# Three running sums of a hidden quarter written back into their PSUM banks, and their low halves formed from there

## The chip, the cores and the metric

The kernel runs on one core of a Trainium2 chip. The metric is the device time of one execution in microseconds. The kernel before takes 2179.87 us (median of three runs, 2179.35 to 2181.54).

## What is computed

Sparse attention over 4 batches, 8 heads, 768 positions and a head width of 64 feeds a mixture of 8 experts on 3072 tokens of width 512. The expert weights of every token come from a gate that is balanced eight times. The change lies in the expert part:

```python
def _moe_ref(x, w_gate, w1, w2):
    ...                                   # P: the balanced gate, tokens x experts
    for e in range(E):                    # 8 experts
        h = np.maximum(x @ w1[e], 0.0)    # 3072 x 512 by 512 x 1024
        ye = h @ w2[e]                    # 3072 x 1024 by 1024 x 512
        out += P[:, e:e + 1] * ye
```

## The kernel before

The attention comes first (to about 550 us, with the first expert work from about 400 us between), then the experts. Expert work is cut into 32 items `i`, one for each expert and batch, and an item into four quarters `qi` of 128 hidden rows. Every float32 factor is held as two float16 parts, a high half and a low half, and one product is three matmuls for each slice (high by high, high by low, low by high).

**First layer, `stage1(i, qi)`.** x @ w1 is a 2x2 block product done with seven products instead of eight. For a quarter, `product(p)` puts product p into one PSUM bank, a tile named `p`: six matmuls of 384 columns (line 1580). The products come in the order 0, 1, 5, 6, 3, 4, 2; from item 8 on product 0 is not done here but is itself split into seven smaller products by `fine` (tiles `fx`, `fy`, `fz`), one item ahead. The banks come from the pool `ps_h`, which has four for all of these; a second pool of four banks, `ps_y`, serves the second layer (tiles `py`).

VectorE's `comb` (line 1485) adds a product to a running sum. The running sums are `a1`, `r11`, `u3` and `c21`, float32 tiles in SBUF of 128x384. Four of them end as blocks of the hidden layer: `r11` after product 1, `c21` after product 3, `u3` after product 4, `a1` after product 2. Each then gets its ReLU on ScalarE (lines 1630, 1663, 1650, 1655).

**Halves of h.** The second layer is a 2x2 block product too, so it needs seven left factors, h 0 to 6. Three are blocks themselves (h 0 from `r11`, h 1 from `c21`, h 3 from `u3`); h 6, 5, 4 and 2 are sums and differences of blocks, which `add` makes on GpSimd (line 1658 and, through `sub`, 1298). `emit(p, src)` makes the two float16 halves: the high half on ScalarE (line 1596), the low half as source minus high half. The low half is done on GpSimd where p is in `LOPE`, else on VectorE, as a TENSOR_TENSOR (both line 1607), or, where `relu=True` is given, as a SCALAR_TENSOR_TENSOR that takes the ReLU along (line 1601).

**Second layer, `stage2(i, p)`.** 36 matmuls of 256 columns (line 1710) for each p, in three groups of 12, in the order 1, 0, 5, 6, 3, 4, 2. The results are added to the output by VectorE (line 1734).

**What sets the order.** The items are interleaved: `stage2` of item i runs between the products of `stage1` of item i + 1. Small work (low halves, sums, the split of the next expert's weights, lines 1276 on ScalarE, 1280 on VectorE, 1291 on GpSimd) waits in the queues of `Slots`, which gives it out by due steps and by planned costs on each engine (`dve=`, `act=`, `pool=`). After that a scheduler of the framework sets the final order on each engine, and it decides which freed bank a new tile of a pool gets.

Of the kernel before, what the change touches and what calls it, by code (L numbers as in the profile page):

```python
# [15 lines left out]
AF = mybir.ActivationFunctionType  # L16
# [18 lines left out]
LGAT = 400  # L35
NU = 8
LOP = (2, 3)
LOPE = (2, 3, 5)
NLE = 99
LEADS, LAGS = (1.0, 1.0, 1.0), (1.0, 1.0, 1.0)  # L40
SD = (2, 3, 4, 5)
# [15 lines left out]
def tile_sparse_attention_moe(  # L57
# [11 lines left out]
    nc = tc.nc  # L69
# [394 lines left out]
    with ExitStack() as actx:  # L464
        pool = lambda name, bufs, **kw: actx.enter_context(
            tc.tile_pool(name=name, bufs=bufs, reuse_waits="tile", **kw)
        )
# [795 lines left out]
    slots = Slots()  # L1263
# [33 lines left out]
    def sub(out, x, y):  # L1297
        nc.gpsimd.tensor_tensor(out=out, in0=x, in1=y, op=ALU.subtract)  # L1298
# [185 lines left out]
    def comb(t, ps, other):  # L1484
        nc.vector.scalar_tensor_tensor(  # L1485
            out=t, in0=ps, scalar=HDOWN, in1=other, op0=ALU.mult, op1=ALU.add
        )
# [83 lines left out]
    def stage1(i, qi, used=None):  # L1571
        fs = slice(qi * P, (qi + 1) * P)
        lop = LOPE if i < NLE else LOP

        def product(p):
            slots.need(("w1", i // B, p))
            ps = ps_h.tile([P, 512], F32, tag="ph", name=f"p{p}_{i}_{qi}")[:, :TH]
            for kc in range(KH):
                for m, (l, r) in enumerate(((0, 0), (0, 1), (1, 0))):
                    nc.tensor.matmul(  # L1580
                        ps, lhsT=w1ps[i // B][p][:, l, kc, fs], rhs=xp[p][:, r, kc],
                        start=(kc == 0 and m == 0), stop=(kc == KH - 1 and m == 2),
                    )
            if used and p in used:
                used[p]()
            return ps

        def fresh(nm):
            return upool.tile([P, TH], F32, tag="u", name=f"{nm}_{i}_{qi}")

        def emit(p, src, relu=False, delay=0):
            key = ("h", i, p), i, qi

            def high():
                h = hs[i, p, qi] = hfree.pop(0)
                nc.scalar.activation(h[:, 0], src, AF.Relu if relu else AF.Copy)  # L1596

            def low():
                h = hs[i, p, qi]
                if relu:  # L1600
                    nc.vector.scalar_tensor_tensor(
                        out=h[:, 1], in0=src, scalar=0.0, in1=h[:, 0],
                        op0=ALU.max, op1=ALU.subtract,
                    )
                else:
                    eng = nc.gpsimd if p in lop else nc.vector
                    eng.tensor_tensor(out=h[:, 1], in0=src, in1=h[:, 0], op=ALU.subtract)  # L1607

            if delay:
                slots.add(high, key, delay, act=0.52)  # L1610
            else:
                high()
            if p in lop:
                slots.add(low, key, delay, pool=0.95)
            else:
                slots.add(low, key, delay + 1, dve=0.6 if relu else 0.78)

        def tick(n, m):
            slots.tick(0.976, 0.55 * n, 0.5 * m)

        if i < FIRST_FINE:
            a1 = fresh("a1")
            nc.scalar.activation(a1, product(0), AF.Copy, scale=HDOWN)
            tick(0, 1)
            yield
        else:
            a1 = pairs[i][qi // 2][:, qi % 2]
        r11 = fresh("r11")
        comb(r11, product(1), a1)
        nc.scalar.activation(r11, r11, AF.Relu)  # L1630
        emit(0, r11)
        tick(1, 2)
        yield
        comb(a1, product(5), a1)
        tick(1, 0)
        yield
        u3 = fresh("u3")
        comb(u3, product(6), a1)
        tick(1, 0)
        yield  # L1640
        slots.settle(i, qi - 1)
        c21 = fresh("c21")
        comb(c21, product(3), u3)
        emit(1, c21, relu=True)
        tick(1, 1)
        yield
        p5 = product(4)
        comb(u3, p5, u3)
        comb(a1, p5, a1)
        nc.scalar.activation(u3, u3, AF.Relu)  # L1650
        emit(3, u3)
        tick(2, 2)
        yield
        comb(a1, product(2), a1)
        nc.scalar.activation(a1, a1, AF.Relu)  # L1655

        def add():
            nc.gpsimd.tensor_tensor(out=s1, in0=a1, in1=u3, op=ALU.add)  # L1658
            sub(a1, a1, r11)
            slots.need((("h", i, 0), i, qi))  # L1660
            sub(r11, s1, r11)
            slots.need((("h", i, 1), i, qi))
            nc.scalar.activation(c21, c21, AF.Relu)
            sub(c21, c21, r11)

        s1 = fresh("s1")
        slots.add(add, (("sum", i), i, qi), 1, act=0.52, pool=4.3)
        emit(4, s1, delay=SD[0])
        emit(6, a1, delay=SD[1])
        emit(5, r11, delay=SD[2])  # L1670
        emit(2, c21, delay=SD[3])
        tick(1, 1)
        yield
# [100 lines left out]
    parts = split_w2(0, wr[2])  # L1774
    parts[0]()
    run(stage1(0, 0))
    for part in parts[1:]:
        part()
    for qi in range(1, FH // P):
        if qi == FH // P - 1:  # L1780
            slots.need(("w2", 0, 1))
        run(stage1(0, qi))
# [6 lines left out]
    def products(i):  # L1789
        def swap(i):  # L1790
            e, b = divmod(i, B)
            return follows[e + 1] if b == B - 1 and e + 1 < NE else None

        if i == FIRST_FINE:
            for _ in fine(i, swap(i)):
                yield 3
        ahead = fine(i + 1, swap(i + 1)) if FIRST_FINE <= i < NI - 1 else None
        for qi in range(FH // P):
            for _ in stage1(i, qi, swap(i) if qi == FH // P - 1 else None):
                yield 2  # L1800
                if ahead and qi >= QFINE and next(ahead, "end") != "end":
                    yield 0
        if ahead:
            for _ in ahead:
                yield 0
# [91 lines left out]
```

## Time and profile before

| | |
|---|---|
| median of three runs | 2179.87 us |
| the profiled execution | 2178.01 us |
| its span on the core | 2176.2 us |
| TensorE matmuls | 2131.4 us busy |
| VectorE | 1793.5 us busy |
| GpSimd | 1481.0 us busy |
| ScalarE | 1278.7 us busy |

The profile lists, for each engine, how long it was busy and what ended its idle time. TensorE's weight loads (PEld) overlap its matmuls (PE). A group of instructions is named by its line, its engine, and the tiles that it writes and reads: `h<-r,h` on line 1607 is the low half made from `r11`.

### The profile page before, as it was taken

To read this page: it belongs to the slowest core of one execution; us is meant where nothing else is said; L and a number is where in the kernel's file an instruction comes from. 1 tells how busy PE (TensorE), PEld (TensorE's weight loads), DVE (VectorE), ACT (ScalarE), POOL (GpSimd) and SP (SyncE) were. 2 spreads that over 40 slices of the span, in tenths; PEclk is the share of its full clock that TensorE was granted. 3 is DMA by queue.
4 is the path that set the end of the run, shared out by engine and by line. 5 is a ranking of instruction groups with operands and counts; after the bars stand their busy time and mean duration, and the time that the engine had idled before them with its cause. 6 is when DMAs were issued, how large, how long until landed. Compare 5 with 4: busy or idle time off the path is not lost.

```text
span 2176.2 us, 48599 instructions
## 1 busy us (share of the span) xinstructions
PE 2131.4 (98%) x19228; PEld 1617.1 (74%) x19228; DVE 1793.5 (82%) x3116; ACT 1278.7 (59%) x2352; POOL 1481.0 (68%) x1550
## 2 busy tenths in 40 slices
PE   6999999999999999999999999999999999999999
PEld 4777776677777777777777777777777777777777
DVE  8889988777878787878787878787878887888775
ACT  5888888766465656555555555555555555555442
POOL 5667778578558775867586758675867586758553
PEclk9999999999999999999999999999999999999999
DMA  6857795142144434343434343434343434343331
GB/s 172 190 127 176 172 214 139 50 135 103 56 155 143 149 117 163 124 155 117 155 117 156 117 156 117 156 117 155 117 155 117 155 117 156 117 156 124 117 103 52
DMA packets 208313, 293.11 MB, mean 135 GB/s; under 512 B 133820, under 2 KB 152276, under 8 KB 200916
## 3 DMA queue, kind: packets, MB, share of 16 engines
q1 hardware_dynamic: 207520, 289.97, 42.4%
q8 instruction: 150, 2.46, 0.5%
q14 instruction: 79, 0.65, 0.1%
q10 hardware_dynamic: 564, 0.03, 0.0%
HBM read 195.59 MB, written 62.91 MB: 119 GB/s over the span
## 4 chain that ended last, share of the span: by engine, by line
PE 67%; DVE 14%; POOL 11%; issue 5%; ACT 4%; DMA 0%; POOLq 0%; DVEq 0%; ACTq 0%
PE py L1710 29%; PE p L1580 24%; PE u L834 3%; POOL h L1607 2%; PE t L769 2%; PE t L772 2%; PE m L736 2%; PE m L739 2%; DVE h L1607 2%; POOL s L1658 2%; DVE top L745 2%; POOL r L1291 1%; DVE acc L1734 1%; DVE w2p L1280 1%; DVE a L1485 1%
## 5 line engine op out<-in xcount | busy, mean ns | idle before, releaser
L1710 PEld LDWEIGHTS <-h 128*128 128x128 f16 x8064 | 787.4, 98 | 155.7 <-issue 9.0
L1710 PE MATMUL py<-w2p,h 128*128 128x256 f16 x4608 | 573.7, 273 | 1.0 <-ACT acc L1731 0.7
L1607 POOL TENSOR_TENSOR h<-u,h 128x384 f16<-128x384 f32 x128 | 135.5, 1059 | 448.6 <-ACT h L1596 448.2
L1710 PE MATMUL py<-vault,h 128*128 128x256 f16 x3456 | 411.2, 273 | 5.2 <-DVE vault L1280 3.1
L1734 DVE SCALAR_TENSOR_TENSOR acc<-py,spare,acc 128x256 f32<-128x256 f32 (+1 forms) x588 | 297.3, 513 | 70.8 <-PE py L1710 64.4
L1596 ACT ACTIVATE h<-c 128x384 f16<-128x384 f32 x256 | 133.0, 521 | 303.4 <-DVE c L1485 232.0
L1580 PEld LDWEIGHTS <-attic 128*128 128x128 f16 x2016 | 196.7, 98 | 104.5 <-issue 0.2
L1485 DVE SCALAR_TENSOR_TENSOR a<-p,a 128x384 f32<-128x384 f32 x384 | 210.8, 549 | 23.6 <-PE p L1580 17.1
L1580 PE MATMUL p<-attic 128*128 128x384 f16 x1152 | 214.4, 326 | 0.0
L745 DVE TENSOR_REDUCE top<-m 128x1 f32<-128x768 f32 x192 | 182.0, 950 | 30.8 <-PE m L739 29.7
L777 ACT ACTIVATE pe<-t,qk 128x768 int32<-128x768 f32 x192 | 172.4, 900 | 57.8 <-PE t L772 45.3
L1580 PEld LDWEIGHTS <-arena 128*128 128x128 f16 x1440 | 140.4, 98 | 77.9 <-issue 4.2
L1658 POOL TENSOR_TENSOR s<-a,u 128x384 f32<-128x384 f32 x128 | 153.7, 1201 | 54.5 <-ACT a L1655 54.2
L1580 PEld LDWEIGHTS <-w1p 128*128 128x128 f16 x1344 | 131.0, 98 | 71.5 <-issue 2.0
L1607 DVE TENSOR_TENSOR h<-s,h 128x384 f16<-128x384 f32 x128 | 114.5, 895 | 68.2 <-ACT h L1596 66.7
L1298 POOL TENSOR_TENSOR c<-c,r 128x384 f32<-128x384 f32 x128 | 158.1, 1235 | 10.0
L1580 PE MATMUL p<-arena,attic 128*128 128x384 f16 x864 | 161.8, 326 | 0.0
L1596 ACT ACTIVATE h<-s 128x384 f16<-128x384 f32 x128 | 66.8, 522 | 161.7 <-POOL s L1658 161.5
L1298 POOL TENSOR_TENSOR r<-s,r 128x384 f32<-128x384 f32 x128 | 153.4, 1199 | 10.0
L1596 ACT ACTIVATE h<-r 128x384 f16<-128x384 f32 x256 | 130.7, 518 | 49.6 <-POOL r L1298 46.4
L1580 PE MATMUL p<-arena 128*128 128x384 f16 x864 | 159.2, 326 | 0.4 <-DVE u L1485 0.2
L791 POOL TENSOR_SCALAR pl<-pe 128x768 f16<-128x768 uint16 x126 | 109.0, 867 | 66.7 <-ACT pe L777 57.9
(239 smaller groups left out, 4732.0 us busy)
## 6 DMA issues: line engine op xcount, KB each, us to landing
arena<-xd SPq DMA_DIRECT2D x128, 384.0 KB, 4.0
accd<-acc SPq DMA_DIRECT2D x28, 1536.0 KB, 5.7
acc<-accd SPq DMA_DIRECT2D x28, 1536.0 KB, 6.5
attic<-xd SPq DMA_DIRECT2D x96, 384.0 KB, 3.7
r<-in_moe_w_dram SPq DMA_DIRECT2D x14, 2048.0 KB, 8.7
xpf<-xfd SPq DMA_DIRECT2D x24, 384.0 KB, 3.1
arena<-in_q_dram SPq DMA_DIRECT2D x16, 384.0 KB, 4.0
arena<-in_k_dram SPq DMA_DIRECT2D x16, 384.0 KB, 4.8
```

The source lines that it names most:

```text
L745: nc.vector.tensor_reduce(out=tops[n][:, c : c + 1], in_=sc[:, :S], axis=AX.X, op=ALU.max)
L777: nc.scalar.activation(pe, sc[:, :S], AF.Exp, bias=EXP_SHIFT, scale=qk[n // 2][3])
L791: nc.gpsimd.tensor_scalar(lo, low, FINE, 1.0, ALU.mult, ALU.mult)
L834: nc.tensor.matmul(uv[:, c, :n], lhsT=l[:, c * P : (c + 1) * P], rhs=w[:, h, kc, :n], start=(kc == 0 and c == 0 and m == 0), stop=(kc == N ...
L1298: nc.gpsimd.tensor_tensor(out=out, in0=x, in1=y, op=ALU.subtract)
L1485: nc.vector.scalar_tensor_tensor(out=t, in0=ps, scalar=HDOWN, in1=other, op0=ALU.mult, op1=ALU.add)
L1580: nc.tensor.matmul(ps, lhsT=w1ps[i // B][p][:, l, kc, fs], rhs=xp[p][:, r, kc], start=(kc == 0 and m == 0), stop=(kc == KH - 1 and m == 2),)
L1596: nc.scalar.activation(h[:, 0], src, AF.Relu if relu else AF.Copy)
L1607: eng.tensor_tensor(out=h[:, 1], in0=src, in1=h[:, 0], op=ALU.subtract)
L1658: nc.gpsimd.tensor_tensor(out=s1, in0=a1, in1=u3, op=ALU.add)
L1710: nc.tensor.matmul(py, lhsT=hs[i, p, kc][:, l, tsl], rhs=w2p[p][:, r, kc], start=(old is None and kc == 0 and m == 0), stop=(kc == KF // 2 ...
L1734: nc.vector.scalar_tensor_tensor(out=dst, in0=src, scalar=c, in1=dst, op0=ALU.mult, op1=ALU.add)
```

## The change

`comb` now writes three of the four finished sums into the PSUM bank that it has just read: the sum of product 1 (until now `r11`), of product 3 (`c21`) and of product 4 (`u3`). High and low halves of h 0, 1 and 3 are formed from the bank, both with the ReLU taken along, and a separate ScalarE instruction puts the ReLU of the sum into the SBUF tile that `add` reads later. The ReLU of `c21` is issued at once and no longer inside `add`. At product 4 the two sums change places, since the one in place has to come second. `LOPE` goes from (2, 3, 5) to (2, 5, 6): the low half of h 3 moves from GpSimd to VectorE, that of h 6 from VectorE to GpSimd. Two planned costs are adapted.

```diff
-LOPE = (2, 3, 5)
+LOPE = (2, 5, 6)
...
-                slots.add(low, key, delay + 1, dve=0.6 if relu else 0.78)
+                slots.add(low, key, delay + 1, dve=0.56 if relu else 0.78)
...
         r11 = fresh("r11")
-        comb(r11, product(1), a1)
-        nc.scalar.activation(r11, r11, AF.Relu)
-        emit(0, r11)
+        p2 = product(1)
+        comb(p2, p2, a1)
+        emit(0, p2, relu=True)
+        nc.scalar.activation(r11, p2, AF.Relu)
         tick(1, 2)
...
         c21 = fresh("c21")
-        comb(c21, product(3), u3)
-        emit(1, c21, relu=True)
-        tick(1, 1)
+        p3 = product(3)
+        comb(p3, p3, u3)
+        emit(1, p3, relu=True)
+        nc.scalar.activation(c21, p3, AF.Relu)
+        tick(1, 2)
         yield
         p5 = product(4)
-        comb(u3, p5, u3)
         comb(a1, p5, a1)
-        nc.scalar.activation(u3, u3, AF.Relu)
-        emit(3, u3)
+        comb(p5, p5, u3)
+        nc.scalar.activation(u3, p5, AF.Relu)
+        emit(3, p5, relu=True)
         tick(2, 2)
...
             slots.need((("h", i, 1), i, qi))
-            nc.scalar.activation(c21, c21, AF.Relu)
             sub(c21, c21, r11)
...
-        slots.add(add, (("sum", i), i, qi), 1, act=0.52, pool=4.3)
+        slots.add(add, (("sum", i), i, qi), 1, pool=4.3)
```

On VectorE, in a plain quarter (item 16, from the low half of h 1 in quarter 1 to product 6 of quarter 2; in `p4_16_1_...` 4 is the product, 16 the item, 1 the quarter), there stood before:

```order
L1601 SCALAR_TENSOR_TENSOR h_5_8119<-c21_16_1_19108,h_5_8119 128x384
L1734 SCALAR_TENSOR_TENSOR acc_1_8145<-py_15_0_1_18932,spare_6_16783,acc_1_8145 128x512
L1485 SCALAR_TENSOR_TENSOR u3_16_1_19082<-p4_16_1_19134,u3_16_1_19082 128x384
L1485 SCALAR_TENSOR_TENSOR a1_16_0_18535<-p4_16_1_19134,a1_16_0_18535 128x384
L1485 SCALAR_TENSOR_TENSOR a1_16_0_18535<-p2_16_1_19146,a1_16_0_18535 128x384
L1734 SCALAR_TENSOR_TENSOR acc_1_8145<-py_15_0_2_18955,spare_6_16783,acc_1_8145 128x512
L1485 SCALAR_TENSOR_TENSOR r11_16_2_19176<-p1_16_2_19177,a1_16_1_18536 128x384
L1607 TENSOR_TENSOR h_8_8122<-s1_16_1_19155,h_8_8122 128x384
L1734 SCALAR_TENSOR_TENSOR acc_1_8145<-py_15_3_0_19189,spare_6_16783,acc_1_8145 128x256
L1607 TENSOR_TENSOR h_24_8138<-a1_16_0_18535,h_24_8138 128x384
L1485 SCALAR_TENSOR_TENSOR a1_16_1_18536<-p5_16_2_19220,a1_16_1_18536 128x384
L1607 TENSOR_TENSOR h_15_8129<-r11_16_2_19176,h_15_8129 128x384
```

and now:

```order
L1601 SCALAR_TENSOR_TENSOR h_5_8119<-p3_16_1_19109,h_5_8119 128x384
L1485 SCALAR_TENSOR_TENSOR a1_16_0_18535<-p4_16_1_19135,a1_16_0_18535 128x384
L1485 SCALAR_TENSOR_TENSOR p4_16_1_19135<-p4_16_1_19135,u3_16_1_19082 128x384
L1485 SCALAR_TENSOR_TENSOR a1_16_0_18535<-p2_16_1_19147,a1_16_0_18535 128x384
L1601 SCALAR_TENSOR_TENSOR h_4_8118<-p4_16_1_19135,h_4_8118 128x384
L1736 SCALAR_TENSOR_TENSOR acc_1_8145<-py_15_0_2_18955,spare_6_16784,acc_1_8145 128x512
L1485 SCALAR_TENSOR_TENSOR p1_16_2_19177<-p1_16_2_19177,a1_16_1_18536 128x384
L1607 TENSOR_TENSOR h_8_8122<-s1_16_1_19156,h_8_8122 128x384
L1736 SCALAR_TENSOR_TENSOR acc_1_8145<-py_15_3_0_19189,spare_6_16784,acc_1_8145 128x256
L1601 SCALAR_TENSOR_TENSOR h_15_8129<-p1_16_2_19177,h_15_8129 128x384
L1485 SCALAR_TENSOR_TENSOR a1_16_1_18536<-p5_16_2_19220,a1_16_1_18536 128x384
```

The low half from `a1` (`h_24`) is gone from VectorE, that of h 3 (`h_4`) has come, and the low halves of h 0 and h 3 read the banks `p1` and `p4`, one or three rows after the sum was written there.

At a change of expert (the first quarters of item 17, while the second layer of item 16 runs with new weights) VectorE also splits w2: `w2p_6` and `vault_110` on line 1280 are the low halves of the weights for products 6 and 5 of the second layer. Before:

```order
L1485 SCALAR_TENSOR_TENSOR a1_17_0_19208<-p2_17_0_19712,a1_17_0_19208 128x384
L1280 SCALAR_TENSOR_TENSOR w2p_6_8110<-r2_4_18992,sw2_4_18997,w2p_6_8110 128x1024
L1280 SCALAR_TENSOR_TENSOR vault_110<-r2_4_18992,sw2_4_18997,vault_110 128x1024
L1485 SCALAR_TENSOR_TENSOR r11_17_1_19741<-p1_17_1_19742,a1_17_0_19208 128x384
L1485 SCALAR_TENSOR_TENSOR a1_17_0_19208<-p5_17_1_19754,a1_17_0_19208 128x384
```

and now:

```order
L1485 SCALAR_TENSOR_TENSOR a1_17_0_19209<-p2_17_0_19713,a1_17_0_19209 128x384
L1485 SCALAR_TENSOR_TENSOR p1_17_1_19742<-p1_17_1_19742,a1_17_0_19209 128x384
L1601 SCALAR_TENSOR_TENSOR h_23_8137<-p4_17_0_19682,h_23_8137 128x384
L1485 SCALAR_TENSOR_TENSOR a1_17_0_19209<-p5_17_1_19753,a1_17_0_19209 128x384
L1280 SCALAR_TENSOR_TENSOR w2p_6_8110<-r2_4_18993,sw2_4_18998,w2p_6_8110 128x1024
L1280 SCALAR_TENSOR_TENSOR vault_110<-r2_4_18993,sw2_4_18998,vault_110 128x1024
```

Three rows more stand ahead of the two splits. On TensorE, at the same place, the second layer's product 5 (`py_16_0_...` on `vault_110`), which needs the second split, followed product 3 of quarter 1; now product 4 comes between:

```order
L1580 MATMUL p4_17_1_19831<-attic_106 128x384
L1580 LDWEIGHTS attic_106
L1580 MATMUL p4_17_1_19831<-attic_106 128x384
L1712 LDWEIGHTS h_10_8124
L1712 MATMUL py_16_0_0_19591<-vault_110,h_10_8124 128x256
```

Product 4 (six matmuls, the last two are shown) has moved ahead of `py_16_0_0`; the same happens at five changes of expert.

## Rows read from the trace of the kernel before

**Rows 1.** The page: busy time, share of the span and instructions of each engine.
```profile
PE 2131.4 (98%) x19228; PEld 1617.1 (74%) x19228; DVE 1793.5 (82%) x3116; ACT 1278.7 (59%) x2352; POOL 1481.0 (68%) x1550
```

**Rows 2.** Busy time by stretch, that of the experts alone (x: instructions).
```profile
core 0: us, PE busy (x) PEld busy (x) DVE busy (x) ACT busy (x) POOL busy (x), PEclk, DMA share, GB/s
550.00:2100.00 1550.00, 1539.21 (x12281) 1185.08 (x12282) 1276.28 (x2211) 838.59 (x1662) 1065.57 (x999) 1.00 0.39 134
```

**Rows 3.** TensorE's waits from 550 to 2100 us: total, times, longest.
```profile
PE py L1710 <- DVE vault L1280: 3.1, 6, 0.5
PE p L1580 <- DVE r L1485: 1.6, 1, 1.6
...
PE fy L1513 <- DVE t L1485: 0.6, 1, 0.6
```

**Rows 4.** Groups by line and shape: busy us, mean ns of one, idle before.
```profile
L1485 DVE SCALAR_TENSOR_TENSOR a<-p,a 128x384 f32<-128x384 f32 x384 | 210.8, 549 | 23.6 <-PE p L1580 17.1
L1607 POOL TENSOR_TENSOR h<-r,h 128x384 f16<-128x384 f32 x128 | 148.1, 1157 | 1.1 <-ACT h L1596 0.3 <-PE py L1710 0.3 <-PE p L1580 0.3
L1607 POOL TENSOR_TENSOR h<-u,h 128x384 f16<-128x384 f32 x128 | 135.5, 1059 | 448.6 <-ACT h L1596 448.2
L1596 ACT ACTIVATE h<-r 128x384 f16<-128x384 f32 x256 | 130.7, 518 | 49.6 <-POOL r L1298 46.4
L1607 DVE TENSOR_TENSOR h<-a,h 128x384 f16<-128x384 f32 x128 | 123.1, 962 | 7.0 <-ACT h L1596 6.3
L1607 DVE TENSOR_TENSOR h<-r,h 128x384 f16<-128x384 f32 x128 | 119.7, 935 | 16.7 <-ACT h L1596 15.9
L1601 DVE SCALAR_TENSOR_TENSOR h<-c,h 128x384 f16<-128x384 f32 x128 | 88.3, 689 | 33.7 <-ACT h L1596 33.5
L1623 ACT ACTIVATE a<-p 128x384 f32<-128x384 f32 x32 | 15.2, 474 | 1.1 <-PE p L1580 1.1
```

**Rows 5.** Timeline, item 16, quarter 1: start us, us, instruction [idle before <-releaser].
```profile
1294.02 1.34 DVE L1607 TENSOR_TENSOR h<-r,h 128x384 f16<-128x384 f32 x1
1294.91 1.23 POOL L1607 TENSOR_TENSOR h<-r,h 128x384 f16<-128x384 f32 x1
...
1298.82 0.56 DVE L1601 SCALAR_TENSOR_TENSOR h<-c,h 128x384 f16<-128x384 f32 x1 [1.32 <-ACT h L1596]
```

**Rows 6.** Timeline at the change of expert, item 17.
```profile
1342.04 2.11 PE L1580 MATMUL p<-arena 128*128 128x384 f16 x12
1342.20 1.00 DVE L1601 SCALAR_TENSOR_TENSOR h<-c,h 128x384 f16<-128x384 f32 x1
...
1343.59 1.27 DVE L1280 SCALAR_TENSOR_TENSOR w2p<-r,sw,w2p 128x1024 f16<-128x1024 f32 x1
...
1344.78 2.11 DVE L1280 SCALAR_TENSOR_TENSOR vault<-r,sw,vault 128x1024 f16<-128x1024 f32 x1
1344.80 1.01 POOL L1658 TENSOR_TENSOR s<-a,u 128x384 f32<-128x384 f32 x1 [2.01 <-ACT a L1655]
...
1345.76 1.90 POOL L1607 TENSOR_TENSOR h<-u,h 128x384 f16<-128x384 f32 x1
...
1345.94 0.49 PE L1710 MATMUL py<-vault,h 128*128 128x256 f16 x3
...
1346.95 2.78 PE L1710 MATMUL py<-vault,h 128*128 128x256 f16 x24 [0.52 <-DVE vault L1280]
...
1347.47 0.56 DVE L1485 SCALAR_TENSOR_TENSOR a<-p,a 128x384 f32<-128x384 f32 x1
```

**Rows 7.** Timeline at the change of expert, item 9.
```profile
902.40 1.14 PE L1580 MATMUL p<-attic,w1p 128*128 128x384 f16 x6
...
903.93 1.35 DVE L1280 SCALAR_TENSOR_TENSOR vault<-r,sw,vault 128x1024 f16<-128x1024 f32 x1
...
906.80 0.86 DVE L1601 SCALAR_TENSOR_TENSOR h<-c,h 128x384 f16<-128x384 f32 x1
907.58 0.55 DVE L1485 SCALAR_TENSOR_TENSOR a<-p,a 128x384 f32<-128x384 f32 x1
```

## The prediction

> **What bounds the kernel now.** I read the page's busy times first: TensorE's matmuls fill 98% of the span, VectorE 82%, GpSimd 68%, ScalarE 59% [rows 1]. The stretches say where the other 2% lie. Of the 1550 us in which the experts alone run, TensorE is busy 1539.2 us at the full clock, so 10.8 us are idle [rows 2]; the rest of the span's 44.8 us (2176.2 - 2131.4) lies outside it, nearly all where the attention runs, which the change leaves alone. The change takes no matmul away. All it can win is idle time of TensorE, and all it can lose is new idle time.
>
> How much idle time that is must be read with care, since the ends of matmuls are modelled. At a change of expert three matmuls of 256 columns are shown as 0.49 us and 24 as 2.78 us; (2.78 - 0.49) / 21 gives 0.109 us for each further one, so three take 0.33 us of the engine, and 0.16 us of the row is the tail of the last [rows 6]. The next matmul starts 1.01 us after the first of the three, so TensorE lost 0.68 us there, where the view shows 0.52 us. TensorE's waits in this stretch come to 10.0 us in 15 places (those on VectorE of 0.6 us and more stand in the rows) [rows 3]. With 0.16 us more for each the ceiling of any gain here is about 10.8 + 15 x 0.16 = 13 us, 0.6% of the time. VectorE ends most of these waits: 6.5 us in 12 places, of which 3.1 us in six places are waits for the split of w2 (line 1280).
>
> **The change part by part.** There are 128 quarters (32 items by 4), and everything below happens once in each.
>
> VectorE, low halves. That of h 6 leaves: 128 x 962 ns = 123.1 us. That of h 3 comes, read from PSUM. No row shows a low half read from PSUM; the nearest is the sum that reads a bank and an SBUF tile of the same shape, at 549 ns [rows 4], so + 70.3 us. That of h 0 falls from 935 to 549 ns, - 49.4 us, and that of h 1 from 689 to 549 ns, - 17.9 us. The means of the SBUF forms are high because single ones are drawn out: 1.34 us where a GpSimd instruction runs beside it, 0.56 us where none does [rows 5]. Sum: - 123.1 + 70.3 - 49.4 - 17.9 = - 120 us.
>
> VectorE, sums in place. No row shows VectorE writing to PSUM. Bounds from the nearest rows: dearer by 689 - 549 = 140 ns, the dearest mean of such an instruction here, or cheaper by the 44 ns by which ScalarE's copy from a bank (474 ns) undercuts its copy from SBUF (518 ns) [rows 4]. For 384 sums that is + 54 to - 17 us; I take nothing, since the shape and the two inputs are those of the 549 ns row. The same 140 ns on the three low halves would be + 54 us more. VectorE thus sheds between 137 and 12 us, I take 120: from 82% to about 75% busy in the expert stretch.
>
> [...] The rows show no penalty for a PSUM source: the sum that reads PSUM takes 549 ns, the undisturbed low half from SBUF 0.56 us [rows 4, 5]. [...]
>
> GpSimd swaps h 3 (135.5 us) for h 6. Its nearest row is the low half of h 5 at 1157 ns, 148.1 us; so 0 to + 13 us [rows 4]. h 5 and h 2 come up to 1.2 us later behind it. That costs nothing as long as the second layer's products 1 and 0 of the same item cover it: 72 matmuls by 0.109 us, 7.8 us, stand between the last product of the first layer and the first use of h 5.
>
> ScalarE keeps its count: three ReLUs and three high halves in a quarter, now all from PSUM. 768 x 44 ns is 34 us less [rows 4]; the other end is no change. ScalarE is at 59% and ends hardly any wait of TensorE that this touches. The order within a quarter does matter: the two ScalarE reads of a bank (0.47 to 0.52 us each [rows 4]) come one after the other, and VectorE's low half after both. For h 0 that is as long as before; for h 1 the low half comes one ReLU later.
>
> Banks. Until now a bank was free when the sum had read it. Now the banks of products 1, 3 and 4 are held through two ScalarE instructions and the low half, about 0.5 + 0.5 + 0.55 = 1.5 us longer, plus what is queued on VectorE. A product takes 0.98 us of TensorE (two in 2.11 us, less the tail of 0.16) [rows 6], and with four banks three other products, often with groups of the second layer between, come before the bank is needed: 2.9 us at the least, so these holds are covered, if VectorE is not late. But the build also gives the banks of products 2 and 5 out sooner, since they come free first. Two kinds of places are tight. At item 9 product 5 of quarter 1 now takes the bank that product 2 of quarter 0 held, one product (0.98 us) later. In five items (13, 17, 21, 25, 29) product 4 of quarter 1 takes the bank of product 5, two products (1.95 us) later.
>
> **The terms of the sum, on TensorE's path.**
> First, the wait for the split of w2, 0.68 us at a change of expert. TensorE's need comes 0.98 us later, because product 4 now stands ahead. VectorE has three rows of 0.55 us more ahead of the two splits, and its low half of h 1 falls from 1.00 to 0.55 us [rows 6]: the split ends 1.65 - 0.45 = 1.20 us later. The wait becomes 0.68 + 1.20 - 0.98 = 0.90 us. If GpSimd no longer draws the second split out (its low half of h 3 at 1345.76 us beside the split is gone), the split takes 1.27 instead of 2.11 us and the wait is 0.06 us. If ScalarE's two instructions for h 3, which now come ahead of the high halves of the split, set the pace, it is some 1.5 us. Five times: - 3.1 to + 4 us; I take - 0.5, near no change, since GpSimd still has its sum at 1344.80 us beside the split.
> Second, the other waits for VectorE's sums, 1.6 and 0.6 us with 0.16 us each, 2.5 us [rows 3]: - 2.5 to + 2.5; I take half away, - 1.3, for 8% less work ahead of them.
> Third, the tight banks. At item 9 product 2 ended on TensorE at 903.54 us, and its sum began at 907.58 and took 0.55 us, 4.6 us later [rows 7]. As late as that, TensorE would stand 4.6 - 0.98 = 3.6 us. In the new order one split (1.35 us) and the low half of h 1 (0.86 us there) come after this sum and not ahead of it, which leaves 1.4 us: + 1.4, from 0 to + 3.6. In the five other items the sum of product 5 ended 3.9 us after the product (1348.03 against 1344.15), 1.9 us too late for the new place; but both splits, 3.4 us, now come behind it [rows 6]. I take 0, from 0 to 5 x 1.9 = + 9.6.
> Sum: - 0.5 - 1.3 + 1.4 = - 0.4 us, with ends at - 5.6 and + 19.7 if all went one way.
>
> The profiled execution took 2178.01 us (span 2176.2 and 1.8 around it); 2177.6 is what the sum makes of it. The median of the runs lies 1.9 us above the profiled execution, so the measured median should come at 2177.6 to 2179.5; I say **2178.5 us**, no change.
>
> **The rivals.**
> *VectorE's relief is what counts (faster).* If low halves and sums all come earlier, the 6.5 us in 12 places that VectorE ends go, with 12 x 0.16 us: 8.4 us, and the time is 2170. For it: VectorE falls behind TensorE by 4 us at the changes of expert [rows 6, 7], and the change takes 120 us off it. Against it: at these very places three more rows now stand ahead of the splits.
> *The banks (slower).* Each bank is used by two engines in turn for longer, and VectorE, late as in the trace before, frees the banks of products 2 and 5 too late: 3.6 + 9.6 us and nothing won, less what overlaps, about + 10 us: 2188.5. It decides from the point where a sum ends more than 0.98 us (item 9) or 1.95 us (five items) behind its product. For it: lags of 3.9 and 4.6 us at the same places [rows 6, 7]. Against it: the new order puts the splits behind these sums. [...]
> *The relief doesn't come.* In-place sums and low halves cost the upper end, VectorE sheds 12 us, GpSimd gains nothing. Then only the first and third terms are left, at + 0.22 x 5 = + 1.1 and + 1.4: about 2181, still no change. [...]
>
> **How the numbers follow.** A measurement of this kernel can tell about 0.2% (4.4 us) from no change, so faster is below 2175.5 and slower above 2184.2. Chances: the forecast 0.46, the relief that doesn't come 0.08 (both within), VectorE's relief 0.26, the banks 0.20. So 0.26 faster, 0.54 the same, 0.20 slower. The range reaches to the two rivals on either side, 2170 to 2188, and leaves out the ends at which everything goes one way.
>
> **What would show it right or wrong.** TensorE's idle time from 550 to 2100 us should stay between 8 and 16 us. `p<-p` sums and `h<-p` low halves on VectorE at about 550 ns, with busy time near 1670 us, show the relief; 690 ns would show that it did not come. The wait of `py` for `vault` (line 1280) should be there still, five or six times. Waits of `p` for VectorE rows of line 1485 or 1601 of over 1 us in the quarters after a change of expert would be the banks. If the idle time falls below 5 us, the relief was underrated.

## The result: 18 us faster, and the profile after

The changed kernel takes 2161.7 us (median of four runs, 2161.35 to 2162.28) against 2180.07 (2179.35 to 2181.54), a ratio of 0.9915 with a 95% interval of 0.9898 to 0.9932. The forecast of no change at 2178.5 was wrong, and the time lies below the range's low end of 2170. The profiled execution went from 2178.01 to 2162.28 us, its span from 2176.2 to 2160.5.

First the page's busy times of the changed kernel, which answer [rows 1]:

```profile
PE 2126.5 (98%) x19228; PEld 1617.8 (75%) x19228; DVE 1680.3 (78%) x3116; ACT 1223.6 (57%) x2352; POOL 1401.6 (65%) x1550
```

VectorE shed 1793.5 - 1680.3 = 113 us, ScalarE 55 us, GpSimd 79 us. The busy time by stretch answers [rows 2]; the experts run alone from 550 us on, and the stretch ends 15 us earlier now:

```profile
core 0: us, PE busy (x) PEld busy (x) DVE busy (x) ACT busy (x) POOL busy (x), PEclk, DMA share, GB/s
0.00:550.00 550.00, 520.84 (x6372) 376.28 (x6373) 466.00 (x836) 415.90 (x651) 379.00 (x525) 1.00 0.59 149
550.00:2085.00 1535.00, 1533.54 (x12267) 1183.66 (x12265) 1171.04 (x2199) 787.32 (x1658) 995.00 (x998) 1.00 0.39 135
```

TensorE is idle for 1535.00 - 1533.54 = 1.5 us of this stretch, where it was 10.8 us. Its waits there are now only these three (total, times, longest, in us), where the prediction counted 15 places [rows 3]:

```profile
PE fx L1513 <- ACT t L1535: 0.6, 1, 0.6
PE cs L1405 <- DVE spare L1399: 0.5, 1, 0.5
PE py L1712 <- DVE vault L1280: 0.4, 1, 0.4
```

None is a wait for a sum of a product, and the wait for the split of w2 is there once instead of six times. The groups by line of the changed kernel answer [rows 4] (busy us, mean ns of one, idle before):

```profile
L1601 DVE SCALAR_TENSOR_TENSOR h<-p,h 128x384 f16<-128x384 f32 x384 | 211.2, 550 | 51.0 <-ACT h L1596 20.0 <-ACT r L1632 19.8 <-ACT c L1647 7.6
L1596 ACT ACTIVATE h<-p 128x384 f16<-128x384 f32 x384 | 186.4, 485 | 249.6 <-DVE p L1485 249.1
L1485 DVE SCALAR_TENSOR_TENSOR p<-p,u 128x384 f32<-128x384 f32 x256 | 143.0, 559 | 44.6 <-PE p L1580 44.0
L1607 DVE TENSOR_TENSOR h<-s,h 128x384 f16<-128x384 f32 x128 | 112.8, 881 | 40.0 <-ACT h L1596 38.4
L1280 DVE SCALAR_TENSOR_TENSOR vault<-r,sw,vault 128x1024 f16<-128x1024 f32 x21 | 27.9, 1330 | 0.6 <-ACT vault L1276 0.6
```

The low half still waits for ScalarE's second read of the bank: 27.4 us of VectorE's idle time before it end with `ACT r L1632` and `ACT c L1647`.

All 384 low halves from PSUM take 550 ns in the mean; the one that VectorE still reads from SBUF (`h<-s`) takes 881 ns. A dearer PSUM source is not seen: 550 ns stands beside the 0.56 us of the undisturbed SBUF form [rows 5].

**Where the time came from.** The view of idle time leaves out the tail of a last matmul (0.16 us), so I counted the trace itself: the time from the start of each matmul to the start of the next, less what its columns take at a granted clock of 1.00 (the median between starts is 0.109 us for 256 columns and 0.162 us for 384), where that is over 0.02 us. From 550 us on this gives 31 gaps of 15.8 us before and 5 gaps of 2.2 us after. Split up: 5.9 us went from 1000 us on (the five changes of expert that repeat; the split of w2 had 5 x 0.68 = 3.4 us of it), 7.7 us between 550 and 1000 us (the first items), and 3.0 us before 550 us, where the first experts run beside the attention. That is 16.6 us, and the span fell by 15.7.

What made the gaps go is seen in how late VectorE is. From the end of a product on TensorE to the start of its sum on VectorE (696 sums from 550 us on) it was 0.76 us in the median and over 3.27 us for one in ten; now it is 0.11 and 1.47 us. 93 sums began more than 2.9 us late before, 2 do now.

The change of expert at item 17, which answers [rows 6], in the timeline of the changed kernel (start us, us, instruction):

```profile
1330.69 2.11 PE L1580 MATMUL p<-arena 128*128 128x384 f16 x12
...
1330.85 0.55 DVE L1601 SCALAR_TENSOR_TENSOR h<-p,h 128x384 f16<-128x384 f32 x1
...
1333.31 1.28 DVE L1280 SCALAR_TENSOR_TENSOR w2p<-r,sw,w2p 128x1024 f16<-128x1024 f32 x1
...
1333.88 1.14 ACT L1276 ACTIVATE w2p<-t,sw 128x1024 f16<-128x1024 f32 x1
...
1334.51 1.28 DVE L1280 SCALAR_TENSOR_TENSOR vault<-r,sw,vault 128x1024 f16<-128x1024 f32 x1
1334.59 1.14 PE L1580 MATMUL p<-attic 128*128 128x384 f16 x6
1334.91 0.52 ACT L1658 ACTIVATE a<-a 128x384 f32<-128x384 f32 x1
...
1335.51 1.15 POOL L1661 TENSOR_TENSOR s<-a,u 128x384 f32<-128x384 f32 x1 [4.30 <-ACT a L1658]
1335.56 2.67 PE L1712 MATMUL py<-vault,h 128*128 128x256 f16 x23
```

The second split takes 1.28 us and not 2.11: GpSimd has no low half of h 3 beside it any more, and GpSimd's sum starts only 0.28 us before the split ends. In both kernels that sum waits for ScalarE's ReLU of `a1`. It comes later against the split because the ReLU now stands behind ScalarE's third split of w2 and not ahead of it, as in the kernel before:

```profile
1344.21 0.51 ACT L1655 ACTIVATE a<-a 128x384 f32<-128x384 f32 x1
...
1345.04 1.13 ACT L1276 ACTIVATE w2p<-t,sw 128x1024 f16<-128x1024 f32 x1
```

TensorE comes to the second layer at 1335.56 and starts it without a wait. Three matmuls, 0.33 us, ran there before the first that waited for the split in the old trace, so the split's end at 1335.79 is about 0.1 us in time.

### The profile page after: what moved, and what is told of

Same layout as the page of the kernel before. It is cut to its first block, busy times and chain, and to the rows that moved or that the text cites. A ratio compares the mean times of both kernels' runs of the same rounds, so it can differ in the third digit from the quotient of the medians.

```text
span 2160.5 us, 48393 instructions
## 1 busy us (share of the span) xinstructions
PE 2126.5 (98%) x19228; PEld 1617.8 (75%) x19228; DVE 1680.3 (78%) x3116; ACT 1223.6 (57%) x2352; POOL 1401.6 (65%) x1550
## 4 chain that ended last, share of the span: by engine, by line
PE 88%; DVE 5%; POOL 3%; ACT 2%; issue 1%; DMA 0%; POOLq 0%; ACTq 0%; DVEq 0%
PE py L1712 39%; PE p L1580 34%; PE u L834 3%; PE t L769 2%; PE t L772 2%; PE m L736 2%; PE m L739 2%; DVE top L745 2%; PE fy L1513 2%; PE fz L1513 1%; PE fx L1513 1%; ACT pe L777 1%; DVE vl L645 1%; POOL s L1661 0%; DVE pl L787 0%
## 5 line engine op out<-in xcount | busy, mean ns | idle before, releaser
L1712 PEld LDWEIGHTS <-h 128*128 128x128 f16 x8064 | 787.8, 98 | 144.6 <-issue 0.5
L1712 PE MATMUL py<-w2p,h 128*128 128x256 f16 x4608 | 571.1, 273 | 0.0
L1661 POOL TENSOR_TENSOR s<-a,u 128x384 f32<-128x384 f32 x128 | 146.8, 1147 | 578.1 <-ACT a L1658 578.0
L1712 PE MATMUL py<-vault,h 128*128 128x256 f16 x3456 | 410.6, 273 | 0.4 <-DVE vault L1280 0.4
L1596 ACT ACTIVATE h<-p 128x384 f16<-128x384 f32 x384 | 186.4, 485 | 249.6 <-DVE p L1485 249.1
L1601 DVE SCALAR_TENSOR_TENSOR h<-p,h 128x384 f16<-128x384 f32 x384 | 211.2, 550 | 51.0 <-ACT h L1596 20.0
L1485 DVE SCALAR_TENSOR_TENSOR p<-p,u 128x384 f32<-128x384 f32 x256 | 143.0, 559 | 44.6 <-PE p L1580 44.0
L834 PE MATMUL u<-vq,pl 128*128 128x65 f16 x1152 | 142.5, 193 | 1.3 <-POOL pl L791 0.9
L1580 PE MATMUL p<-arena,w1p 128*128 128x384 f16 x768 | 143.7, 326 | 0.0
```

What stands on the lines that cost most here:

```text
L834: nc.tensor.matmul(uv[:, c, :n], lhsT=l[:, c * P : (c + 1) * P], rhs=w[:, h, kc, :n], start=(kc == 0 and c == 0 and m == 0), stop=(kc == N ...
L1485: nc.vector.scalar_tensor_tensor(out=t, in0=ps, scalar=HDOWN, in1=other, op0=ALU.mult, op1=ALU.add)
L1580: nc.tensor.matmul(ps, lhsT=w1ps[i // B][p][:, l, kc, fs], rhs=xp[p][:, r, kc], start=(kc == 0 and m == 0), stop=(kc == KH - 1 and m == 2),)
L1601: nc.vector.scalar_tensor_tensor(out=h[:, 1], in0=src, scalar=0.0, in1=h[:, 0], op0=ALU.max, op1=ALU.subtract,)
L1712: nc.tensor.matmul(py, lhsT=hs[i, p, kc][:, l, tsl], rhs=w2p[p][:, r, kc], start=(old is None and kc == 0 and m == 0), stop=(kc == KF // 2 ...
```

## The experiments

All against the kernel before on the same chip. "Gaps" are counted as above, in us, for three stretches of the span; "half" is what matmuls at the half clock (granted 0.50) cost on top from 550 us on (explained at the run e10_once_more; in e4_product_4, e9_other_plan and e12_h6_back_gpsimd the clock fell before 550 us, and the 1.5 to 1.7 us stand under the gaps 50-550); "late" are sums of the 696 that begin more than 2.9 us after their product. Busy times are in us. Some runs do work twice with the same values, which adds load and leaves the output as it is.

| run | median us | ratio (95%) | VectorE | GpSimd | gaps 50-550 | 550-1000 | from 1000 | half | late |
|---|---|---|---|---|---|---|---|---|---|
| before | 2180.1 | 1 | 1793.5 | 1481.0 | 18.8 | 9.9 | 5.9 | 0 | 93 |
| after | 2161.7 | 0.9915 (0.9898-0.9932) | 1680.3 | 1401.6 | 15.8 | 2.2 | 0 | 0 | 2 |
| e1_swap_only | 2181.8 | 1.0013 (1.0004-1.0022) | 1759.7 | 1461.2 | 17.5 | 10.5 | 9.8 | 0 | 69 |
| e2_h6_back | 2168.0 | 0.9949 (0.9934-0.9964) | 1760.4 | 1329.4 | 15.5 | 2.6 | 5.4 | 0 | 21 |
| e3_products_1_3 | 2168.8 | 0.9952 (0.9937-0.9967) | 1715.2 | 1445.6 | 18.6 | 5.0 | 0.3 | 0 | 19 |
| e4_product_4 | 2176.6 | 0.9990 (0.998-1.0) | 1743.1 | 1454.1 | 23.7 | 3.0 | 6.3 | 0 | 65 |
| e5_vector_more | 2179.3 | 0.9996 (0.9987-1.0006) | 1791.9 | 1406.7 | 16.6 | 7.2 | 9.5 | 1.7 | 14 |
| e6_low_from_sbuf | 2181.6 | 1.0008 (0.9999-1.0018) | 1745.4 | 1462.0 | 16.8 | 7.3 | 9.9 | 1.7 | 31 |
| e7_gpsimd_more | 2168.2 | 0.9946 (0.9931-0.9961) | 1695.1 | 1532.0 | 15.9 | 4.9 | 2.9 | 0 | 16 |
| e8_three_banks | 2194.6 | 1.0068 (1.0051-1.0085) | 1683.1 | 1401.9 | 17.0 | 11.0 | 21.5 | 0.9 | 10 |
| e9_other_plan | 2160.9 | 0.9915 (0.9900-0.9930) | 1681.4 | 1406.8 | 16.1 | 1.6 | 0 | 0 | 0 |
| e10_once_more | 2166.1 | 0.9941 (0.9926-0.9956) | 1741.6 | 1407.1 | 16.1 | 3.2 | 1.4 | 1.6 | 3 |
| e11_before_plan | 2178.2 | 0.9995 (0.9985-1.0004) | 1793.5 | 1480.3 | 20.1 | 11.6 | 1.4 | 1.4 | 72 |
| e12_h6_back_gpsimd | 2170.9 | 0.9962 (0.9948-0.9976) | 1761.4 | 1468.8 | 19.9 | 1.4 | 4.8 | 0 | 40 |

The four columns of a row, added up and held against those of before (34.6), give each run's difference in time within 2.4 us, so they tell where the time is.

**Which part of the change is it?** First the two halves of GpSimd and VectorE swapped, and nothing else:

```diff
-LOPE = (2, 3, 5)
+LOPE = (2, 5, 6)
```

> The kernel before with LOPE = (2, 5, 6) alone: the low half of h 3 on VectorE, that of h 6 on GpSimd, everything still read from SBUF. Theory load (TensorE waits because VectorE's queue is behind, and the change won by taking 113 us off VectorE): one low half goes and one of the same kind comes, VectorE stays near 1785 us busy, so about as before, 2176 to 2182 us. Rival placement (what counts is which engine has which low half, not PSUM): most of the gain is there, 2162 to 2168.

Nothing is won: 2.5 us slower, though VectorE is 34 us less busy. TensorE's waits in this run, from 550 us on:

```profile
PE py L1710 <- DVE acc L1734: 7.1, 9, 1.1
PE py L1710 <- DVE vault L1280: 2.7, 5, 0.6
```

The five waits for the split are there as before, though the split takes 1.27 us in this run: it starts later. Others have come, for additions to the output.

The changed kernel without the swap's second half, so that VectorE keeps h 6 and GpSimd has two low halves:

```diff
-LOPE = (2, 5, 6)
+LOPE = (2, 5)
```

> The changed kernel with LOPE = (2, 5): the low half of h 6 back on VectorE, all else as changed, so the three sums and low halves still use PSUM. VectorE gets some 120 us back (about 1800 us busy, as before the change), GpSimd loses about 130. Theory load: the gain goes, 2175 to 2182 us. Rival form (what counts is that low halves from PSUM are short and aren't drawn out beside GpSimd, not the sum of VectorE's work): the gain stays, 2160 to 2166.

The gain falls from 18.4 to 11.3 us. With 80 us more on VectorE the wait for the split is back, with gaps of 1.07 to 1.09 us at each of the five changes (`PE py L1712 <- DVE vault L1280` is the only large wait), and the first items stay mended. But TensorE's order is another here too: at item 17 the second layer's product 5 stands behind product 1 of quarter 1 and not behind product 4, four products earlier. So this run does not tell the load from the order.

Only the sums of products 1 and 3 in place, with their halves and early ReLU, on the kernel before (this run and the next also have the change's planned costs for what they take over; only the main lines are shown):

```diff
-        comb(r11, product(1), a1)
-        nc.scalar.activation(r11, r11, AF.Relu)
-        emit(0, r11)
+        p2 = product(1)
+        comb(p2, p2, a1)
+        emit(0, p2, relu=True)
+        nc.scalar.activation(r11, p2, AF.Relu)
...
-        comb(c21, product(3), u3)
-        emit(1, c21, relu=True)
+        p3 = product(3)
+        comb(p3, p3, u3)
+        emit(1, p3, relu=True)
+        nc.scalar.activation(c21, p3, AF.Relu)
...
```

> Only the sums of products 1 and 3 in place, with h 0 and h 1 from PSUM; product 4 and LOPE as before. VectorE sheds about 65 us (to about 1728 us busy). Theory load: over half of the gain, 2166 to 2173 us. Rival placement: no gain, 2178 to 2182.

10.5 us are won, more than half, with the old distribution of low halves. Only product 4 in place, with the swap:

```diff
-LOPE = (2, 3, 5)
+LOPE = (2, 5, 6)
...
-        comb(u3, p5, u3)
         comb(a1, p5, a1)
-        nc.scalar.activation(u3, u3, AF.Relu)
-        emit(3, u3)
+        comb(p5, p5, u3)
+        nc.scalar.activation(u3, p5, AF.Relu)
+        emit(3, p5, relu=True)
```

> Only the sum of product 4 in place, h 3 from PSUM on VectorE, with LOPE = (2, 5, 6). VectorE sheds about 50 us (to about 1740 us busy). Theory load: under half of the gain, 2170 to 2177 us. Rival placement: all of it, 2160 to 2166.

2.8 us are won. 10.5 and 2.8 don't make 18.4: the parts help each other.

**Is it the source of the low halves, or the sums in place?** The changed kernel with everything left as it is, but the three low halves formed on VectorE from the SBUF tiles that hold the ReLU:

```diff
-                    nc.vector.scalar_tensor_tensor(
-                        out=h[:, 1], in0=src, scalar=0.0, in1=h[:, 0],
-                        op0=ALU.max, op1=ALU.subtract,
-                    )
+                    nc.vector.tensor_tensor(
+                        out=h[:, 1], in0=done, in1=h[:, 0], op=ALU.subtract
+                    )
...
-        emit(0, p2, relu=True)
+        emit(0, p2, relu=True, done=r11)
```

> The changed kernel with one thing undone: the three low halves are taken from the SBUF tiles r11, c21 and u3 (which ScalarE has written with the ReLU), as TENSOR_TENSOR; sums in place, high halves from PSUM and LOPE stay. Theory form: the gain goes, 2176 to 2184 us, with the low halves at 850 to 950 ns. Theory sums (the gain comes from the rest of the change: the early ReLU of c21, sums and high halves in PSUM): it stays, 2161 to 2167 us. Theory load expects some 2175 us, as VectorE gets about 100 us back.

The whole gain is gone: the time is that of before (1.9 us more, with an interval that reaches 1). The run with the swap alone, which has none of the sums in place, high halves from PSUM and early ReLUs, stood at 2.5 us more. So these bring next to nothing by themselves; the low half's source is the part that the gain needs. Its groups:

```profile
L1601 DVE TENSOR_TENSOR h<-r,h 128x384 f16<-128x384 f32 x128 | 113.0, 882 | 29.5 <-ACT r L1631 28.9
L1601 DVE TENSOR_TENSOR h<-u,h 128x384 f16<-128x384 f32 x128 | 82.6, 645 | 21.5 <-ACT h L1596 19.2
L1601 DVE TENSOR_TENSOR h<-c,h 128x384 f16<-128x384 f32 x128 | 80.5, 629 | 12.9 <-ACT c L1646 12.5
```

That is 276 us instead of 211 us for the same 384 low halves. The edit also changes the kind of instruction, but those of them that lie beside no GpSimd instruction take 549 to 558 ns in the mean here too (counted in the trace), so the kind is not what costs. And its waits on TensorE:

```profile
PE py L1711 <- DVE w2p L1280: 7.0, 5, 1.4
PE py L1711 <- ACT vault L1276: 2.1, 1, 2.1
```

The five waits are for another split than before, the last one of w2 (`w2p` from `r`). That place in the timeline of this run:

```profile
1351.61 4.20 PE L1711 MATMUL py<-w2p,h 128*128 128x256 f16 x37
...
1352.19 0.54 DVE L1485 SCALAR_TENSOR_TENSOR a<-p,a 128x384 f32<-128x384 f32 x1
...
1354.14 0.76 DVE L1601 TENSOR_TENSOR h<-r,h 128x384 f16<-128x384 f32 x1 [0.94 <-ACT r L1631]
...
1356.77 1.35 DVE L1606 TENSOR_TENSOR h<-s,h 128x384 f16<-128x384 f32 x1
...
1358.04 1.93 DVE L1280 SCALAR_TENSOR_TENSOR w2p<-r,sw,w2p 128x1024 f16<-128x1024 f32 x1
```

and in that of the changed kernel:

```profile
1341.27 0.54 DVE L1485 SCALAR_TENSOR_TENSOR a<-p,a 128x384 f32<-128x384 f32 x1
...
1341.44 4.20 PE L1712 MATMUL py<-w2p,h 128*128 128x256 f16 x37
...
1342.95 0.75 DVE L1736 SCALAR_TENSOR_TENSOR acc<-py,spare,acc 128x512 f32<-128x512 f32 x1 [0.67 <-PE py L1712]
...
1344.82 0.55 DVE L1601 SCALAR_TENSOR_TENSOR h<-p,h 128x384 f16<-128x384 f32 x1
1345.28 0.89 DVE L1607 TENSOR_TENSOR h<-s,h 128x384 f16<-128x384 f32 x1
...
1346.09 2.02 DVE L1280 SCALAR_TENSOR_TENSOR w2p<-r,sw,w2p 128x1024 f16<-128x1024 f32 x1
...
1348.53 1.36 PE L1712 MATMUL py<-w2p,h 128*128 128x256 f16 x11
```

From the start of the same 37 matmuls the split ends 1359.97 - 1351.61 = 8.36 us later in the one and 1348.11 - 1341.44 = 6.67 us in the other. TensorE takes the split up some 7.1 us after that start (1348.53), so the changed kernel has about 0.4 us to spare. In this run TensorE is ready 0.25 us sooner, since three of the six `fx` matmuls stand ahead of the 37, and 1.7 us more for the split become a gap of 1.57 us, five times. The 1.7 us can be read off: 0.75 VectorE is late already when the 37 matmuls begin (its sum into `a` starts 0.58 us after them, and 0.17 us before them in the changed kernel); 0.27 it waits longer (0.94 us for ScalarE's ReLU, since the low half stands earlier in this order, against 0.67 us for TensorE); 0.21 and 0.46 its two low halves take longer. These five gaps make 7.9 us of the 17.7 us that this run has more than the changed kernel (the four columns added up). Another 6.8 us lie between 550 and 1000 us, most of them at item 9: the wait of 2.1 us above and 1.7 us at the half clock after it.

**How much does load cost?** The changed kernel with one low half (of h 1), then with two (of h 0 and h 1), made twice from PSUM:

```diff
+                    for _ in range(2 if p == 1 else 1):
                         nc.vector.scalar_tensor_tensor(
```

> The changed kernel with the low half of h 1 alone made twice from the bank: 128 x 0.55 us, VectorE at about 1740 us busy, GpSimd as changed (about 1402). Twice that dose (141 us) took the whole gain. Theory load: about half of the gain goes, 2168 to 2174 us. If the loss comes only past a point (VectorE as full as before): 2162 to 2166 us.

```diff
+                    for _ in range(1 if p == 3 else 2):
                         nc.vector.scalar_tensor_tensor(
```

> The changed kernel with the low halves of h 0 and h 1 made twice on VectorE, each time from the bank (the second writes the same values): 256 x 0.55 us, 141 us, so about 1820 us busy, above the 1793 us before the change. Theory load (VectorE's total work decides): all of the gain goes, 2178 to 2186 us. Theory form (what decides is that instructions with a PSUM source are never held up by GpSimd, so that VectorE's queue keeps to the planned times): most of the gain stays, 2163 to 2170 us.

61 us more on VectorE take 4.6 us off the gain, 112 us more take 18.1 and thereby all of it. (The run with low halves from SBUF has 65 us more on VectorE and loses 20.3: the sum of its work does not explain it.) It is not the sums that come late: with two, 14 begin more than 2.9 us late, where the kernel before had 93 at the same busy time. About half of the loss is the last split again, gaps of 1.61 to 1.63 us at the five changes, 8.1 us; 6.7 us more lie between 550 and 1000 us, a stall of 2.5 us at 881.6 us and 1.7 us at the half clock after it among them. The waits on TensorE of the run with two:

```profile
PE py L1713 <- DVE w2p L1280: 7.3, 5, 1.5
PE p L1580 <- DVE a L1485: 2.6, 2, 2.3
```

With one the split still makes it, and most of the 4.6 us stem from one place at item 9, in that run's timeline:

```profile
896.44 1.15 ACT L1276 ACTIVATE vault<-r,sw 128x1024 f16<-128x1024 f32 x1 [1.66 <-POOL r L1291]
...
897.64 0.49 PE L1713 MATMUL py<-vault,h 128*128 128x256 f16 x3 [2.00 <-ACT vault L1276]
...
899.37 2.13 PE L1580 MATMUL p<-arena,attic 128*128 128x384 f16 x6
```

GpSimd gives the remainder for the split late, TensorE stands for 2.2 us, and after it six matmuls of 384 columns take 2.13 us instead of 1.14. The busy time of a piece of that stretch shows why; the granted clock (third from the end) is 0.50:

```profile
899.50:901.00 1.50, 1.50 (x7) 0.66 (x6) 1.22 (x3) 1.05 (x3) 1.50 (x2) 0.50 0.00 0
```

That is the "half" of the table: 1.6 us on top of the stall.

Load on GpSimd instead, the low half of h 2 made twice there, in the changed kernel and in the one with h 6 back on VectorE:

```diff
-                    eng.tensor_tensor(out=h[:, 1], in0=src, in1=h[:, 0], op=ALU.subtract)
+                    for _ in range(2 if p == 2 else 1):
+                        eng.tensor_tensor(out=h[:, 1], in0=src, in1=h[:, 0], op=ALU.subtract)
```

> The changed kernel with the low half of h 2 made twice on GpSimd (the same values again): 128 x 0.92 us, about 118 us, so some 1520 us busy, above the 1481 us before the change. If GpSimd's relief (80 us) was what counted: 2174 to 2182 us. Theories load and form: it stays within 2161 to 2167 us, a little more where GpSimd's longer use holds up VectorE's remaining low half from SBUF.

> The low half of h 6 back on VectorE, as in the run that kept two thirds of the gain at 1760 us of VectorE, and the low half of h 2 made twice on GpSimd, which puts GpSimd at about 1450 us instead of 1329, near what it had where VectorE's 1760 us gave no gain. Theory two loads (both engines' work counts, since VectorE's SBUF instructions are drawn out beside GpSimd and GpSimd's sums come late): 2174 to 2182 us. Theory form (instructions from PSUM keep the gain whatever GpSimd does): 2166 to 2170 us.

130 us more on GpSimd take 6.9 us off the gain, and in the other kernel 139 us take 2.3. At 1532 us GpSimd is busier than before and the kernel still 11.5 us faster, so the relief of GpSimd (79 us) is a part of the gain but not what it rests on.

**Is it the order?** A planned cost of another size gives other places in the queues, with the same work: the changed kernel with 0.78 for 0.56, and the kernel before with 0.56 and 0.95 for its 0.6 and 0.78.

```diff
-                slots.add(low, key, delay + 1, dve=0.56 if relu else 0.78)
+                slots.add(low, key, delay + 1, dve=0.78 if relu else 0.78)
```

> The changed kernel with the planned cost of its short low halves at 0.78 instead of 0.56: no instruction more or less, only the order on the engines differs. This is the control for all other runs, each of which also moves the order. If the gain hangs on a lucky order: 2168 us or more. If VectorE's work decides: 2160 to 2165 us, VectorE near 1680 us busy.

> The kernel before with other planned costs alone (0.56 and 0.95 instead of 0.6 and 0.78): the control for the order of the kernel before. If its time hangs on an unlucky order: 2172 us or less. If VectorE's work decides: 2177 to 2184 us.

The one is 19.0 us faster than before, the changed kernel 18.4; the other is 1.7 us faster, with an interval that reaches 1. The whole gain doesn't hang on one lucky order: another order of before stays near 2180, and another order of after stays at 2161. But a part can be had by order alone: in the other order of before the split of `vault` at item 17 takes 1.27 us and the gaps from 1000 us on fall from 5.9 to 1.4 us, while those ahead of 1000 us grow by 3.0 us, with 1.4 us at the half clock.

**The banks.** The changed kernel with three banks for the first layer's products instead of four:

```diff
-    ps_h = mpool("ps_h", 4, space=PSUM)
+    ps_h = mpool("ps_h", 3, space=PSUM)
```

> The changed kernel with three banks instead of four for the products. The rival of the prediction, that banks held longer stall TensorE, was not seen with four. A bank is now held some 2.5 to 3 us at the median until VectorE's low half has been read (from the changed trace), and with three banks the next use comes after two products, 2 us, or after two products and one or two groups of the second layer, 3.3 to 4.6 us. If banks have little room left: over 2200 us. If they have plenty: 2161 to 2170 us.

33 us slower than with four. The waits on TensorE of this run:

```profile
PE py L1712 <- DVE vault L1280: 8.2, 5, 1.7
PE p L1580 <- DVE h L1601: 4.2, 8, 0.6
PE p L1580 <- DVE a L1485: 3.9, 8, 1.1
```

A product waiting for a low half (`p` for `h`) is a bank held too long, as the rival had it; with four banks the view names no such wait from 550 us on, and one of 0.4 us before.

## Why the prediction was wrong, step by step

- **Sizes of the instructions: right.** The low half from PSUM was put at 549 ns and takes 550; the sum in place at 549 and takes 559 to 561. VectorE was to shed 120 us (from 12 to 137) and shed 113; ScalarE 34, and shed 55. GpSimd was to gain 0 to 13 us and lost 79: I had reckoned its instructions at their old means, but the means of most of them fell (`h<-r` on GpSimd 1157 ns before, 968 after).
- **The ceiling of 13 us: too low.** It rested on 15 waits that the view names, and on the stretch from 550 us on alone. There were 31 gaps, 15.8 us, and before 550 us, where the first experts run, 3.0 us more were won. I had written of the rest of the idle time that the change leaves it alone. The waits were also misread: VectorE ended 8.0 us in 13 places and not 6.5 in 12, for of these lines of the kernel before

```profile
PE p L1580 <- ACT a L1539: 1.7, 1, 1.7
...
PE cs L1405 <- DVE spare L1399: 1.5, 1, 1.5
```

I left the second out, and it fell to 0.5 us. The first is gone too, though no term had it.
- **First term, - 0.5 us for the split: the wrong case taken.** The case of 0.06 us stood there: GpSimd no longer draws the split out. I left it because GpSimd's sum stood beside the split in the trace of before. That sum moved back by 1.0 us against the split, with the ReLU of `a1` that it waits for. The split starts 1.08 us later against product 1 of the quarter (I had 1.20), but takes 0.83 us less. The wait is gone at all five changes, 3.4 us, and 2.5 us more of other gaps from 1000 us on.
- **Second term, - 1.3 us: a size with no reason.** I took half of 2.5 us "for 8% less work". VectorE was not late by its total but by a queue of several us at some places, and that queue shrank by more than the share of work that was taken off it: one sum in ten was over 3.27 us late, now over 1.47, and the first items won 7.7 us. Not all of that is a queue on VectorE: the longest gap there, 1.83 us at 881 us, ends with `ACT a L1539`, which waited 2.09 us for VectorE's line 1466, and that 1.95 us for ScalarE, which had waited 1.84 us for GpSimd.
- **Third term, + 1.4 us for tight banks: nothing.** The banks of products 1, 3 and 4 are held longer, as foreseen (the last read by VectorE comes 2.5 to 3.0 us after the product in the median, where it was 0.8 to 1.7). But I set the lateness of before, 4.6 and 3.9 us, against the new deadlines and took off only the rows that now stand behind the sums. At item 9 the sum of product 2 now begins 0.30 us after it instead of 4.04, at item 17 that of product 5 0.04 instead of 3.32.
- **The rivals.** "VectorE's relief" was the right mechanism at too low a price: 8.4 us, since it counted the 12 places only. "The banks" don't decide with four of them and do with three. My sign for the former, idle time below 5 us, is what the trace shows: 1.5 us.

The failing step is thus the turn from relief to TensorE's waits: three terms that come to - 0.4 us, with the lateness read off the old trace held nearly fixed, though the change took away what made it. In their place the gaps fell by 16.6 us.

**What stays open.** VectorE's total doesn't tell a kernel's time. At 1742 to 1761 us of it, the kernels with three low halves from PSUM take 2166 to 2171 us, those with one or none 2177 to 2182. For the runs with low halves from SBUF and with two made twice the traces show a part of the reason, the last split of w2 missing its place five times: 7.9 of 17.7 us and 8.1 of 17.0 us of gaps. With h 6 back the other split is late because TensorE comes to it four products earlier; why the framework's order has it there I have not traced. Of the 7.9 us that the run with product 4 alone loses before 550 us against the changed kernel, 2.45 us are one stall ahead of a `cs` matmul of the gate at 548.5 us, and 1.7 us are the half clock after a stall of 2.33 us at 335.7 us. The rest of it is open. That SBUF reads drawn out beside GpSimd come in just the places that miss is only argued.

## What to carry to other kernels

When an engine that feeds the bottleneck is late in bursts, don't price its relief by the share of work that goes: ask how late its last result is at each burst, and by how much the place misses or makes its deadline (here 0.4 us to spare, then 1.6 us lost, five times over). Count gaps between starts on the bottleneck, in all stretches where the changed work runs, before naming a ceiling. And a low half read from the bank in which the sum lies was never drawn out here: none of the 384 took more than 559 ns, beside a GpSimd instruction or not.

## What the hardware showed that I had not expected

- VectorE writes a sum back into the bank that it reads at 559 to 561 ns, against 550 ns into SBUF.
- ScalarE's 384 columns take 485 ns from PSUM, and 522 to 524 ns from SBUF in the same kernel.
- The low halves from PSUM are not drawn out beside GpSimd: 134 of the 384 lay beside a GpSimd instruction for at least nine tenths of their time and took 548 ns in the mean. Of the low halves of h 1 from SBUF before, 35 lay so and took 942 ns in the mean, and 82 lay beside none and took 553. The means of other instructions fell too, but not of all: VectorE's split of `vault` went from 1638 to 1330 ns without any change to it and GpSimd's `h<-r` from 1157 to 968, while VectorE's split of `w2p` from `r` went from 1495 to 1529 and GpSimd's `a<-a,r` from 1010 to 1069. Of the 128 low halves that VectorE still reads from SBUF in the changed kernel (`h<-s`), 107 lay beside a GpSimd instruction for at least nine tenths of their time and took 920 ns in the mean.
- After a stall of TensorE of 2.16 to 2.75 us the granted clock fell to 0.50 in eight runs (0.9 to 1.7 us lost each): four in the expert stretch, where the kernel before has no stall above 1.83 us, and four during the attention or at its end. After stalls of 2.34 us in the changed kernel, 2.40 and 2.45 us in the runs with the swap and with product 4 alone, and 2.86 us in the run with products 1 and 3 alone, it stayed at 1.00.
